# Attention and a softplus MLP in one kernel: eight heads of scores in one TensorE burst, the first loads over two DMA queues, and the order of work searched anew

## Chip, cores, metric

One Trainium2 chip, one core. The metric is the device time of one execution in microseconds (us), median over several. The span of a profile is some 2 us shorter than that time. The medians given beside them are of all runs; in numbers 1 to 4 below one run of the kernel before is a slow one, and in number 1 one of the edited kernel.

## The reference, cut

```python
# attention: batch 4, heads 8, sequence 768, head size 64; 8 global keys, window of 96
scores = scale * q @ k.T + bias(distance)          # keep: global or 0 <= rel < 96
a = softmax(where(keep, scores, -1e9));  x = a @ v
# the MLP on the 3072 x 512 result
h = x @ w_in                                       # 512 -> 2048
g = maximum(h, 0) + log1p(exp(-abs(h)))            # softplus
out = g @ w_out                                    # 2048 -> 512
```

## The kernel before: the parts that matter

The sequence is cut into 24 blocks of 128 queries (n = 0 to 23), two to a unit of loads and two to a group g of the MLP (12 groups). Every piece of work is an `op` with an engine, a planned duration, a rank, and what it reads and writes. A planner runs these through a small model, and its order is what each engine gets. So a changed number in the plan moves hundreds of instructions. The code is shortened.

```python
LEADS = {3: 2.25, 4: 2, 5: 3, ..., 9: 2, ...}       # how far ahead units are loaded
MARGIN = {-1: 15.0, 0: 13.5, 1: 25.5, 2: -36.5, 3: 1.5}
s_ps = [ps.tile([P, 2, 512], F32, name=f"s_ps{i}") for i in range(2)]   # 2 score tiles of 2 banks
# ...
def scores(n, part, rank):           # part: heads 0-3 or 4-7; 64 rows per matmul
    # ...
    for m in range(2):
        for u in range(u_all):       # own block, and the block before
            for y in range(2):
                # ... (rows: one half of the array; c: columns of the bank)
                nc.tensor.matmul(banks[:, y, c : c + P], kt[rows, 2 * part + m, :], qv(rows, 2 * part + m), ...)
# ...
def soften(n, part, rank):           # DVE adds the bias (z), ScalarE takes exp (pb)
# ...
def mm1(g, p, rank):                 # first product: 8 matmuls to h_ps; then e = exp(h), g = ln(1 + e) on ScalarE
def mm2(g, ns, rank):                # second product: g x w_out
# ...
for part in range(2):
    scores(n, part, rank + 0.1 * part)
    soften(n, part, rank + 0.1 * part)
```

Fillers are 90 matmuls on a blank tile, placed wherever the plan expects TensorE to be idle in the start. All loads are issued on SyncE.

The softmax here doesn't subtract the row's maximum and nothing guards it: scores larger than these inputs give would overflow.

Of the kernel before, what the change touches and what calls it, by code (L numbers as in the profile page):

```python
# [23 lines left out]
class Planner:  # L24
# [162 lines left out]

UNITS = [(0, 0), (1, 0), (0, 1), (0, 2), (1, 1), (1, 2), (2, 0), (2, 1), (2, 2), (3, 0), (3, 1), (3, 2)]
WIDE = (0, 1, 2)
FIRST_LOADS = "q1 k0 q0 i3 i6 i1 i0 k1 o0 i2 v0 v1 i7 i4 i5 o7 o2 q2 o1 o6 o3 o4 o5 k2 v2".split()  # L190
LOAD_LEAD = 2.5
LEADS = {3: 2.25, 4: 2, 5: 3, 6: 3, 7: 2.75, 8: 3, 9: 2, 10: 3.25, 11: 3.25}
FILLERS = 90
TABLE_RANK = -9000.0
BIAS0_ON = ["DVE"]
BIASA_ON = ["ACT"]
PE_BIAS = (0, 1, 3)
PE_KEYS = {
    0: (("o",), ("h0",), ("s", 1, 0), ("o",)),
    1: (("s", 1, 0), ("s", 1, 1), ("s", 1, 0), ("h0",)),  # L200
    2: (("s", 1, 0), ("s", 1, 1), ("x",), ("s", 1, 0)),
}
PE_X = {0: ("h1",), 1: ("o",), 2: ("o",), 3: ("o",), 4: ("x",), 5: ("x",)}
PV_KEYS = {
    (0, 0): ("h0",),
    (0, 1): ("o",),
    (1, 0): ("o",),
    (1, 1): ("h0",),
    (2, 0): ("o",),
    (2, 1): ("o",),  # L210
    (3, 0): ("o",),
    (3, 1): ("o",),
}
O_KEYS = {
    (0, 0): ("s", 1, 0),
    (0, 1): ("s", 0, 0),
    (1, 0): ("s", 1, 1),
    (1, 1): ("o",),
    (10, 1): ("x",),
    (11, 0): ("s", 1, 0),  # L220
}
FINE = 2
NARROW = ()
TAIL = 8.0
ENG = {
    0: {"k": ["POOL", "ACT"], "q": ["POOL", "POOL"], "tk": ["ACT", "ACT"], "tq": ["ACT", "DVE"], "v": ["POOL", "POOL", "DVE", "DVE"]},
    1: {"k": ["ACT", "POOL"], "q": ["DVE", "POOL"], "tk": ["DVE", "ACT"], "tq": ["ACT", "DVE"], "v": ["POOL", "ACT"]},
    2: {"k": ["POOL", "POOL"], "q": ["DVE", "POOL"], "tk": ["DVE", "DVE"], "tq": ["DVE", "ACT"], "v": ["ACT"]},
}
ENG_X = {0: "ACT"}  # L230
ENG_W = {"i3": "DVE"}
NUDGE = {
    "b0.0.10": -4,
    "b0.0.14": -0.5,
    "b0.0.2": -4,
    "b0.0.4": -8,
    "b0.0.6": -8,
    "b0.1.12": 2,
    "b0.1.2": 8,
    "b1.0.2": -4,  # L240
    "b1.1.12": -4,
    "biasTrue1": -8,
    "castk0.0": 4,
    "castk1.0": -4,
    "castk3.00": -8,
    "castk4.00": -2,
    "castq1.1": 4,
    "castq2.0": -2,
    "cin0": 8,
    "cin3": -8,  # L250
    "cpq0.0": 4,
    "cpq0.1": 1,
    "e0.0": 2,
    "e0.3": -8,
    "ex1.1": -4,
    "ldk3": -8,
    "ldk4": -2,
    "ldv4": 2,
    "nm2.0": 8,
    "nm2.1": 4,  # L260
    "nm3.0": -8,
    "nm3.1": -2,
    "pv3.0": 4,
    "sb0.1": -8,
    "sb1.1": -8,
    "sb3.1": -8,
    "sc3.0": -8,
    "sc3.1": 8,
    "trk1.0": -8,
    "wout4": 8,  # L270
    "xt2": -8,
    "xt3": -8,
}
DIST0_ON = "POOL"
S_ON = {
    (0, 0): 1,
    (0, 1): 1,
    (1, 0): 0,
    (1, 1): 0,
    (2, 0): 1,  # L280
    (2, 1): 0,
    (3, 0): 1,
    (3, 1): 0,
    (4, 0): 0,
    (4, 1): 1,
    (5, 0): 0,
    (5, 1): 0,
    (6, 0): 1,
    (6, 1): 1,
    (7, 0): 1,  # L290
    (7, 1): 0,
}
T0 = 47.5
LATER = 38.0
MARGIN = {-1: 15.0, 0: 13.5, 1: 25.5, 2: -36.5, 3: 1.5}
SOONER = {"cin": -36.0, "cout": 12.0}
LAST_KEYS = (("s", 0, 0), ("x",), ("o",))


@with_exitstack  # L300
def kernel(
# [129 lines left out]
    def load_unit(i, rank, only="qkv"):  # L431


        s, b0 = units[i][0]
        sl = slice(P * b0, P * b0 + W)
        for z, which in enumerate(only):
            src = {"q": q, "k": k, "v": v}[which][s]
            slot = raw_slot((which, i))
            raw = raw_t[slot]
            sync = gates.get((which, i), ())  # L440
            if i in WIDE and which != "v":
                for y in range(2):

                    def fn(src=src, raw=raw, y=y):
                        return nc.sync.dma_start(  # L445
                            raw[:, 512 * y : 512 * y + 512],
                            src[y::2, sl, :].rearrange("h (g r) d -> g h (r d)", r=8),
                        )

                    op(f"ld{which}{i}.{y}", "SP", 0.64, rank + 0.01 * z, fn, dma=(0.7, 86.0), sync=sync,  # L450
                       writes=[("raw", slot, y)])
                continue

            def fn(src=src, raw=raw):
                return nc.sync.dma_start(
                    raw[:].rearrange("p (h c) -> p h c", h=H),
                    src[:, sl, :].rearrange("h (p r) d -> p h (r d)", r=2),
                )

            op(f"ld{which}{i}", "SP", 0.45, rank + 0.01 * z, fn, dma=(1.78, 30.0), sync=sync,  # L460
               writes=raw_keys(slot))
# [111 lines left out]
    def transp_pe(i, which, banks, engs, rank):  # L573
# [4 lines left out]
        for rs in ((0, 1),) if len(held(banks)) == 1 else ((0,), (1,)):  # L578

            def mm(rs=rs):  # L580
# [4 lines left out]
                        nc.tensor.matmul(tr[:, a], src[:, c : c + P], ident[:])  # L585

            keys = held([banks[r] for r in rs])
            op(f"tr{which}{i}.{rs[0]}", "PE", 0.24 * len(rs), rank + 0.1 * rs[0], mm, count=4 * len(rs),
               reads=[(which + "b", i % NQB, x) for x in range(4)] + ["ident"], writes=keys)
            eng = engs[rs[0] % len(engs)]  # L590

# [44 lines left out]
               writes=[v_keys(prev)[r]], after=since)  # L636

    def s_of(n, part):
        return S_ON.get((n, part), part)

    def b_keys(n, part):
        return [("bias", blocks[n][1] > 0, h) for h in range(4 * part, 4 * part + 4)]

    def scores(n, part, rank):

        i = blocks[n][1]
        u_all = 2 if i > 0 else 1
        biased = n in PE_BIAS
        banks = s_ps[s_of(n, part)]
        key = ("s", s_of(n, part))  # L650
        qv = q_of(n)

        def seed():
            for y in range(2):
                src = (biasA if i else bias0)[:, part, 2 * u_all * y : 2 * u_all * y + 2 * u_all, :]
                nc.tensor.matmul(  # L656
                    banks[:, y, 0 : 256 * u_all], ident[:], src.rearrange("p a b -> p (a b)"),
                    start=True, stop=False, skip_group_check=True,
                )

        if biased:
            op(f"sb{n}.{part}", "PE", 0.22 * u_all, rank - 0.1, seed, reads=["ident"] + b_keys(n, part),
               writes=[key], count=2)

        def fn():
            for m in range(2):
                for u in range(u_all):
                    kt = kt_of(before(n) if u else n)
                    for y in range(2):
                        rows = slice(64 * y, 64 * y + 64)  # L670
                        c = P * (u_all * m + u)
                        reg = banks[:, y, c : c + P]
                        nc.tensor.matmul(  # L673
                            reg if unit_of(n) in WIDE else reg.rearrange("p (r t) -> p r t", r=2),
                            kt[rows, 2 * part + m, :], qv(rows, 2 * part + m),
                            start=not biased, stop=True, skip_group_check=biased,
                        )

        reads = kt_keys(n) + [("qT", unit_of(n) % NQT, r) for r in range(2)] + (kt_keys(before(n)) if i else [])
        op(f"sc{n}.{part}", "PE", 0.06 + 0.124 * u_all, rank, fn, reads=reads, writes=[key], count=4 * u_all)  # L680

    zi = {}

# [58 lines left out]
    def x_transp(n, key, eng, rank):  # L742
# [4 lines left out]
        if key is not None:  # L747
# [8 lines left out]
            def ev():  # L756
                copy_on[eng](dst, tr)

            op(f"xt{n}", "PE", 0.23, rank, mm, reads=in_keys + ["ident"], writes=held([key]), count=4)
            return op(f"xc{n}", eng, 0.36 if eng == "DVE" else 0.51, rank, ev, writes=[xkey] + held([key]))  # L760
        else:

# [112 lines left out]
                allow_small_or_imprecise_dtypes=True,  # L875
            )

    op("table", "ACT", 1.3, TABLE_RANK, table)
    op("blank", "DVE", 0.25, -9001.0, lambda: nc.vector.memset(blank[:], 0.0), writes=["blank"])  # L879
    op("iota", "POOL", 0.83, -9000.0, iotas, writes=["rel"], count=2)  # L880
    op("ident", "POOL", 0.6, -8999.0, lambda: make_identity(nc, ident), writes=["ident"], count=2)
# [27 lines left out]
    def biases(eng, late, h, rank):  # L909
        f = -slopes[h] * root_d  # L910
        part, at = h // 4, 2 * (h % 2) + h // 2 % 2
        dst, src = (biasA[:, part, 2 * at : 2 * at + 2, :], dist) if late else (bias0[:, part, at, :], dist0)

        def fn():
            if eng == "ACT":
                nc.scalar.mul(dst, src[:], f)
            else:
                (nc.vector if eng == "DVE" else nc.gpsimd).tensor_scalar_mul(dst, src[:], f)

        dur = {"DVE": (0.21, 0.30), "ACT": (0.20, 0.31), "POOL": (0.6, 0.9)}[eng][late]  # L920
        op(f"bias{late}{h}", eng, dur, rank, fn, reads=["dl0", "dl1"] if late else ["d0"],
           writes=[("bias", late, h)], port=eng == "DVE")

    distances(0, -9000.0)
    op("d0", DIST0_ON, 0.25, -8990.0, lambda: copy_on[DIST0_ON](dist0[:], dist[:, 0, :]), reads=["dl0"],
       writes=["d0"], port=DIST0_ON == "DVE")
    op("d0e", "DVE", 0.42, -8980.0, lambda: both(
        lambda sl: v_.tensor_scalar_min(dist0[sl, :], dist0[sl, :], float(NL))), writes=["d0"], count=2, port=True)
# [31 lines left out]
    def attend(n, rank):  # L960
        if blocks[n][1] >= 2:
            since = [placed[before(n)]] if before(n) in placed else []
            globals_k(n, rank, since)
            globals_v(n, rank + 0.3, since)
        for part in range(2):
            scores(n, part, rank + 0.1 * part)
            soften(n, part, rank + 0.1 * part)
        for part in range(2):
            pv(n, part, PV_KEYS.get((n, part), ("x",)), rank + 0.2)
        x_transp(n, PE_X.get(n), ENG_X.get(n, "DVE"), rank + 0.3)  # L970
# [134 lines left out]
```

## Time and profile before

225.42 us (three runs, 225.40 to 225.44).

| | before |
|---|---|
| span | 222.8 us |
| TensorE busy, fillers included | 216.6 us, 97% |
| ScalarE, DVE, POOL busy | 161.7, 107.2, 94.0 us |
| first transpose of q, first group of the first product | 7.55, 22.48 us |
| bursts of score matmuls | 35 |

The prediction below shows the lines and how they are read.

### The profile page before, as it was taken

What the parts mean: (1) busy time and instruction counts of PE and PEld (TensorE: products, weight loads), DVE (VectorE), ACT (ScalarE), POOL (GpSimd) and SP (SyncE); (2) the same over time, 40 slices, a digit from 0 to 9 for tenths busy, and PEclk for the clock granted to TensorE, in tenths of its full rate; (3) what the DMA queues carried; (4) which work ended last, traced back from release to release, by engine and by line L of the source; (5) the groups of instructions that cost most, each with busy time, mean ns of one, the idle gap of its engine ahead of it and who ended that gap; (6) DMA issues with size and microseconds to landing.
All of it is one profiled execution on the core that took longest, in us unless ns stands there. A gap on an engine that the chain in (4) does not pass through costs nothing.

```text
span 222.8 us, 5073 instructions
## 1 busy us (share of the span) xinstructions
PE 216.6 (97%) x2062; PEld 150.7 (68%) x2062; DVE 107.2 (48%) x205; ACT 161.7 (73%) x216; POOL 94.0 (42%) x157
## 2 busy tenths in 40 slices
PE   8899999999998999999999999999999999999994
PEld 5778897665574577767667676657667667767553
DVE  4246365560768767374266268118777621001121
ACT  5676889973399599897589587857987958877300
POOL 4457897593373836406445607748124100000000
PEclk9999999999999999999999999999999999999999
DMA  4999999975999487774999259996622131011112
GB/s 159 310 347 388 385 388 355 296 142 157 301 220 262 81 226 171 151 211 101 270 305 243 76 157 284 175 278 196 118 75 71 26 88 53 3 47 47 47 51 94
DMA packets 69847, 40.96 MB, mean 184 GB/s; under 512 B 30144, under 2 KB 61248, under 8 KB 69824
## 3 DMA queue, kind: packets, MB, share of 16 engines
q1 hardware_dynamic: 69680, 40.58, 69.5%
q8 instruction: 16, 0.26, 0.5%
q10 hardware_dynamic: 144, 0.07, 0.1%
q14 instruction: 7, 0.06, 0.1%
HBM read 27.26 MB, written 6.29 MB: 151 GB/s over the span
## 4 chain that ended last, share of the span: by engine, by line
PE 92%; ACT 2%; DMA 2%; POOL 1%; SPq 1%; DVE 0%; issue 0%
PE h_ps L779 38%; PE o_ps L828 27%; PE s_ps L828 7%; PE s_ps L673 6%; PE x_ps L722 4%; PE x_ps L940 3%; DMA raw<-in_q_dram 2%; PE x_ps L828 2%; PE s_ps L585 1%; ACT g L805 1%; ACT pb L705 1%; POOL vb L633 1%; PE s_ps L656 1%; SPq L445 1%; ACT e L794 1%; PE o_ps L722 1%
## 5 line engine op out<-in xcount | busy, mean ns | idle before, releaser
L779 PE MATMUL h_ps<-XT,w_in_bf 128*128 128x256 bf16 x768 | 96.7, 273 | 0.0
L779 PEld LDWEIGHTS <-w_in_bf 128*128 128x128 bf16 x768 | 72.5, 98 | 16.9
L794 ACT ACTIVATE e<-h_ps 128x512 f32<-128x512 f32 x96 | 59.7, 629 | 31.7 <-PE h_ps L779 31.2
L828 PE MATMUL o_ps<-w_out_bf,g 128*128 128x512 bf16 (+1 forms) x304 | 72.5, 371 | 1.0 <-ACT g L805 0.6
L828 PEld LDWEIGHTS <-g 128*128 128x128 bf16 x416 | 37.7, 98 | 32.5 <-ACT g L805 1.3
L698 DVE TENSOR_TENSOR z<-s_ps,biasA 128x1024 f32<-128x1024 f32 x36 | 43.2, 1220 | 21.5 <-PE s_ps L673 20.0
L805 ACT ACTIVATE g<-e 128x1024 bf16<-128x1024 f32 x48 | 50.7, 1057 | 1.3
L705 ACT ACTIVATE pb<-z 128x1024 bf16<-128x1024 f32 (+1 forms) x42 | 40.9, 987 | 9.0 <-DVE z L698 8.8
L857 DVE COPY osb<-o_ps 128x512 f32<-128x512 f32 (+1 forms) x19 | 12.7, 669 | 46.3 <-PE o_ps L828 46.2
L633 POOL COPY vb<-vb 4x512 bf16<-4x512 bf16 x32 | 20.1, 628 | 28.1 <-PE x_ps L722 27.1
L524 POOL CAST vb<-raw 64x512 bf16<-64x512 f32 x40 | 25.2, 631 | 14.9 <-DMA raw<-in_v_dram 13.3
L524 POOL CAST kb<-raw 64x512 bf16<-64x512 f32 x36 | 22.7, 631 | 20.0 <-DMA raw<-in_k_dram 18.5
L722 PEld LDWEIGHTS <-pb 128*128 128x128 bf16 x352 | 16.6, 98 | 5.3 <-issue 0.4
L733 DVE TENSOR_TENSOR xs<-x_ps,rcp 128x256 bf16<-128x256 f32 x40 | 17.0, 425 | 1.4
L828 PE MATMUL s_ps<-w_out_bf,g 128*128 128x512 bf16 (+1 forms) x80 | 17.0, 358 | 0.0
L722 PE MATMUL x_ps<-vb,pb 128*128 128x65 bf16 x304 | 16.0, 193 | 0.3 <-DVE xs L733 0.2
L940 PE MATMUL x_ps<-blank 128*128 128x256 bf16 x90 | 14.2, 307 | 1.1 <-DVE blank L879 1.1
L732 DVE RECIPROCAL rcp<-x_ps 128x4 f32<-128x4 f32 x40 | 7.1, 177 | 12.1 <-PE x_ps L722 12.1
L940 PEld LDWEIGHTS <-blank 128*128 128x128 bf16 x90 | 9.5, 113 | 3.1 <-DVE blank L879 1.1
L673 PE MATMUL s_ps<-qT,kT 64*128 64x128 bf16 x224 | 10.9, 218 | 0.0
L673 PEld LDWEIGHTS <-kT 64*128 64x128 bf16 x224 | 6.8, 94 | 5.7 <-issue 5.5
L482 POOL CAST w_out_bf<-raw 128x1024 bf16<-128x1024 f32 x8 | 8.3, 1040 | 3.3 <-DMA raw<-in_moe_w_out_dram 3.2
(72 smaller groups left out, 107.9 us busy)
## 6 DMA issues: line engine op xcount, KB each, us to landing
raw<-in_v_dram SPq DMA_DIRECT2D x12, 512.0 KB, 6.0
out_dram<-osb SPq DMA_DIRECT2D x23, 256.0 KB, 2.4
raw<-in_q_dram SPq DMA_DIRECT2D x9, 512.0 KB, 4.4
raw<-in_k_dram SPq DMA_DIRECT2D x9, 512.0 KB, 5.8
raw<-in_moe_w_in_dram SPq DMA_DIRECT2D x8, 512.0 KB, 10.3
raw<-in_moe_w_out_dram SPq DMA_DIRECT2D x8, 512.0 KB, 8.2
raw<-in_k_dram SPq DMA_DIRECT2D x6, 256.0 KB, 5.3
raw<-in_q_dram SPq DMA_DIRECT2D x6, 256.0 KB, 5.3
```

Source lines behind the costliest of these rows:

```text
L524: copy_on[eng](dst, src)
L633: nc.gpsimd.tensor_copy(vb_of(prev)[sl, :, 0:D], vb_of(first)[sl, :, 0:D])
L673: nc.tensor.matmul(reg if unit_of(n) in WIDE else reg.rearrange("p (r t) -> p r t", r=2), kt[rows, 2 * part + m, :], qv(rows, 2 * part + m ...
L698: nc.vector.tensor_tensor(z, src, bias, ALU.add)
L705: nc.scalar.activation(pb[:, 0:nr, :].rearrange("p (y a) b -> p y (a b)", y=2), src, AF.Exp, scale=1.0 / root_d)
L722: nc.tensor.matmul(xv[:, h, :], pb[:, u_all * (2 * (h % 2) + h // 2) + u, :], vb_of(prev if u else n)[:, 4 * part + h, :], start=u == 0, s ...
L733: nc.vector.tensor_tensor(xs[:, 4 * part : 4 * part + 4, :], xv[:, :, 0:D], rcp[:][:, :, None].to_broadcast([P, 4, D]), ALU.mult,)
L779: last = nc.tensor.matmul(hv[:, j, :], w_in_bf[:, m, fb * P : fb * P + P], XT[g % NXG][:, m, :], start=(m == 0), stop=(m == NM - 1),)
L794: nc.scalar.activation(e[:, p % 2, :, :].rearrange("p j (b t r) -> p (j b) r t", b=2, r=2), hb[:].rearrange("p (a r t) -> p a r t", a=4, r=2),
L805: nc.scalar.activation(gt[:, 2 * p - 2 : 2 * p + 2, :].rearrange("p a t -> p (a t)"), e[:].rearrange("p a j t -> p (a j t)"), AF.Ln, bias=1.0,
L828: nc.tensor.matmul(bank(key)[:, 0 : z - a], gt[:, fb, ns * P : ns * P + P], w_out_bf[:, fb, a:z], start=(fb == 0), stop=(fb == NFB - 1),)
L940: nc.tensor.matmul(x_ps[:, 0:256], blank[:, 0:P], blank[:, 0:256])
```

## The change

Intent: write the scores of 15 blocks for all eight heads at once, over both score tiles (four banks), so that TensorE changes its row tiling less often; and bring the first q in over ScalarE's queue while SyncE issues the first k and v. The plan's durations were refitted and its constants searched anew.

```diff
-    def scores(n, part, rank):
+    def scores(n, parts, rank):
...
+            for part in parts:
                 for m in range(2):
...
-        for part in range(2):
-            scores(n, part, rank + 0.1 * part)
-            soften(n, part, rank + 0.1 * part)
+        for parts in ((0, 1),) if n in WHOLE else ((0,), (1,)):
+            scores(n, parts, rank + 0.1 * parts[0])
+            for part in parts:
+                soften(n, part, rank + 0.1 * part)
...
+WHOLE = (0, 4, 6, 7, 8, 9, 10, 12, 13, 14, 15, 16, 17, 18, 23)
+LOAD_ON = {"q0": "ACT"}
...
-LEADS = {3: 2.25, 4: 2, 5: 3, 6: 3, 7: 2.75, 8: 3, 9: 2, 10: 3.25, 11: 3.25}
+LEADS = {3: 2.25, 4: 2.75, 5: 3, 6: 2.75, 7: 2.75, 8: 3.5, 9: 2.25, 10: 2.75, 11: 3.5}
-NARROW = ()
+NARROW = (0,)
-MARGIN = {-1: 15.0, 0: 13.5, 1: 25.5, 2: -36.5, 3: 1.5}
+MARGIN = {-1: 10.5, 0: -15.0, 1: 69.0, 2: 65.5, 3: 21.0}
... (engines of casts and copies, banks, some 200 small shifts of rank: cut)
```

## The prediction

> **What bounds the kernel now.** I read the page's busy table and its slices first, then the chain of waits, then timelines of TensorE, then the waits of the start.
>
> ```profile
> span 222.8 us, 5073 instructions
> PE 216.6 (97%) x2062; PEld 150.7 (68%) x2062; DVE 107.2 (48%) x205; ACT 161.7 (73%) x216; POOL 94.0 (42%) x157
> PEclk9999999999999999999999999999999999999999
> DMA  4999999975999487774999259996622131011112
> ...
> PE 92%; ACT 2%; DMA 2%; POOL 1%; SPq 1%; DVE 0%; issue 0%
> ...
> L940 PE MATMUL x_ps<-blank 128*128 128x256 bf16 x90 | 14.2, 307 | 1.1 <-DVE blank L879 1.1
> ```
>
> TensorE is busy 97% and carries 92% of the chain, at full clock throughout. The DMA engines are full for the first 8 slices of 5.57 us and rarely later. The last line is a warning: 90 of the matmuls multiply a blank tile. They are fillers that keep TensorE running while it has no work, so busy time hides idle time, and all of them lie in the start.
>
> I cut the span by stage. The chain of waits has its first useful matmul (a transpose of q) at 7.55 us and the first group of the first MoE product (8 matmuls to h_ps) at 22.55. A table by stage gives 14.9 of 14.9 us busy from 7.55 to 22.48, of which 62 fillers; back to back a filler takes 0.109 us in the chain ("0.87 ... x_ps L940 x8"), so 6.8 us of that stretch is idle time in disguise. From 22.48 to the last matmul at 219.7 TensorE counts 195.9 us busy of 197.2. The end, from 219.7 to 222.8, is one eviction and one store.
>
> So there are three places to gain: the start, whatever hides inside the busy 197 us, and a few true stalls. For the second, the timeline of TensorE in the middle (columns: start, duration, engine, what, count; a row's duration contains the modelled end of its last matmul, so I use differences of starts):
>
> ```profile
> 80.31 1.04 PE L779 MATMUL h_ps<-XT,w_in_bf 128*128 128x256 bf16 x8
> 81.28 0.40 PE L673 MATMUL s_ps<-qT,kT 64*128 64x128 bf16 x8
> 81.61 0.42 PE L722 MATMUL x_ps<-vb,pb 128*128 128x65 bf16 x8
> 81.87 1.04 PE L779 MATMUL h_ps<-XT,w_in_bf 128*128 128x256 bf16 x8
> 82.74 1.03 PE L828 MATMUL o_ps<-w_out_bf,g 128*128 128x512 bf16 x4
> 83.60 1.04 PE L779 MATMUL h_ps<-XT,w_in_bf 128*128 128x256 bf16 x8
> 84.57 0.62 PE L673 MATMUL s_ps<-qT,kT 64*128 64x128 bf16 x16
> 85.12 0.42 PE L722 MATMUL x_ps<-vb,pb 128*128 128x65 bf16 x8
> ```
>
> The reader is to see the price of entering and leaving the score matmuls. A group of 8 on L779 takes 0.87 us when another full-array group follows (81.87 to 82.74), but 0.97 when scores follow (80.31 to 81.28): 0.10 us to enter. Eight scores take 0.33 (81.28 to 81.61), sixteen take 0.55 (84.57 to 85.12): 0.22 for eight more, so 0.11 us to leave. Two bursts made one save 0.21 us.
>
> For the third, the only large true stall after the start is near 70 us:
>
> ```profile
> 66.67 1.98 ACT L705 ACTIVATE pb<-z 128x1024 bf16<-128x1024 f32 x2
> 68.55 1.04 ACT L805 ACTIVATE g<-e 128x1024 bf16<-128x1024 f32 x1
> 69.65 1.04 PE L828 MATMUL o_ps<-w_out_bf,g 128*128 128x512 bf16 x4
> 70.15 1.06 ACT L805 ACTIVATE g<-e 128x1024 bf16<-128x1024 f32 x1
> 71.26 1.04 PE L828 MATMUL o_ps<-w_out_bf,g 128*128 128x512 bf16 x4 [0.58 <-ACT g L805]
> ```
>
> ScalarE does the two exponentials of a block ahead of the logarithm that TensorE needs. TensorE's starts between 68.3 and 73.1 show about 1.8 us lost over what those matmuls take elsewhere.
>
> **What the Trainium skill says.** "TensorEngine Tiling (Array Packing)", section "Key Properties": changing the tiling mode drains TensorE. The scores use 64 rows and everything around them 128; the 0.10 + 0.11 us above agree. "TensorE: Matmul & The Clock Gate", Part 1, tells of a clock that needs work to stay up; the fillers are there for it, and the granted clock reads full in all slices. "DMA: Bandwidth & Descriptors", section "Issuing engines are not separate DMA queues": transfers from several engines share the same 16 DMA engines, so a second issuer saves only issue time. The trace of before has nearly all loads on one queue and cannot confirm it; it does show the issue time, 0.60 to 0.66 us per half tile.
>
> **The change part by part.**
>
> Scores in one burst. In 15 of 24 blocks the eight heads are written in one go, over both score tiles (four banks). That does not give 15 x 0.21 us: TensorE's timeline of before already has 10 bursts of sixteen where two halves happened to meet, beside 21 of eight, 3 of four and 1 of twelve, 35 bursts in all. After, 15 whole blocks plus 9 blocks in halves make at most 15 + 18 = 33; if a third of the nine pairs still meet, 30. 35 - 30 = 5 bursts x 0.21 = **1.0 us**, on the path, since TensorE has no other slack there (0.4 to 1.5 with 33 to 28 bursts). The matmuls themselves stay 352, and DVE's additions stay 36 of 1.22 us.
>
> The start. Loads in order of issue on SyncE:
>
> ```profile
> 0.73 0.66 SPq L445 DMA_DIRECT2D raw<-in_k_dram  x1
> 1.45 1.22 SPq L445 DMA_DIRECT2D raw<-in_q_dram  x2
> 2.71 1.25 SPq L445 DMA_DIRECT2D raw<-in_k_dram  x2
> 4.01 0.60 SPq L445 DMA_DIRECT2D raw<-in_q_dram  x1
> ...
> 5.95 0.60 SPq L455 DMA_DIRECT2D raw<-in_v_dram  x1
> 6.59 1.36 SPq L480 DMA_DIRECT2D raw<-in_moe_w_in_dram  x2
> ```
>
> q's second half is cast from 6.88, k's second used half from 7.60, v only at 12.46. With both halves of q on ScalarE, SyncE is spared two issues, 2 x 0.63 = 1.25 us, and q can start at 0.7 in place of 1.45. But q and k are 1 MB, and 310 to 390 GB/s (slices 1 to 5) carry 1 MB in about 3 us, so they cannot all be in before some 5.8: I take 1.0 us off the first transpose. ScalarE pays two issues of 0.6 us in a stretch where it waits for data anyway (1.9 us ahead of its first cast). The transposes of unit 0 also go to banks of their own (in before, o_ps serves q and then k, and the second k transposes start at 9.96 for that reason, 1.1 us after the first); some 0.7 us more. v earlier removes the wait of 2.7 us on DVE for it, which counts only as far as the exponentials (to 15.9) no longer cover it.
>
> The weights. In the first column chunk the loads become narrow: one 512 KB tile serves the first group instead of two, so TensorE can begin after 0.5 MB less, 0.5 / 0.385 = 1.3 us of a full DMA. In before the copy of XT ends at 19.95 while the casts of weights run until 21.7, so both the attention path and the weights must move, and I count the smaller: first h_ps group near 20, about 2.5 us earlier. Of that, scores and a bias seed that lay between 20.3 and 22.5 (1.5 us) must be done later, and half of those would fit a filler's place: **1.7 us** net. It is bounded by the 6.8 us of fillers.
>
> The new order of everything else (biases, casts, priorities) has no cost of its own. It can remove the 1.8 us near 70, or make such stalls elsewhere, since whole blocks bring the two exponentials (2.0 us) together more often. I put it at **0.5 us** gained. Sum: 1.0 + 1.7 + 0.5 = 3.2 us; 225.4 - 3.2 = 222.2 us.
>
> **The rivals.** (1) The start is bound by bytes. DMA is at 9 tenths from slice 1 and three units with both weights are 12.5 MB, 32 us at 385 GB/s; an earlier first group then waits for the following weights, and the gain is handed back as idle time between 25 and 40 us. For: the full DMA slices; against: TensorE had work throughout 22 to 44 us while the same bytes came in. It would leave 224. (2) Whole bursts need four free banks and hand ScalarE two exponentials in a row; logarithms come late and stalls like that at 70 us repeat. For: that stall; against: the eight other bursts of sixteen show no such gap. A few of 0.7 us would leave 224 to 226. (3) The reordering is better than I can see: start 3.5 us, bursts 1.5, stall all of 1.8 removed: 218.6.
>
> **Range and chances.** My terms run from 0.4 to 1.5, 0 to 3.5 and -1.5 to 1.8. Not all ends fall together, so 219.6 to 224.9 should hold eight times in ten, about 222.2. Two per cent lies at 220.9, 1.3 us beyond my figure, with a spread of some 2 us: 0.27 for faster. Slower by 2% would need 230, more than all rivals together: 0.04. The rest, 0.69, is within.
>
> **What would show it.** Right: about 30 score bursts, most of sixteen, still 0.10 and 0.11 us at the edges; first useful transpose near 6.5, first h_ps group near 20; fewer than 62 fillers' worth of time after the first transpose; no wait of TensorE for g near 70. Wrong: first group still near 22 (bytes or casts bind), filler time unchanged, or TensorE waiting for ScalarE's g or e several times. Busy time of DVE should stay near 107 us plus some casts, of ScalarE near 160; neither should become the bound.

## More of the kernel before

Later units load q and k, cast them to bf16 (mostly on POOL), and transpose them by DMA.

## The result, and the profile after

222.24 us (four runs, 221.98 to 222.85) against 225.43 us: ratio 0.9858, 95% interval 0.9835 to 0.9881. A ratio is the mean time of one kernel's fast runs over that of the other's of the same rounds, so not quite the ratio of the medians. Executions over 1.5% slower than the fastest of the same kernel are left out of the means. The change is 3.2 us faster, within 2%. On another chip the same kernel gave 0.9887 (0.9855 to 0.9918), number 5 below.

The page of the changed kernel, its busy times and its chain of waits:

```profile
span 219.9 us, 5042 instructions
PE 213.5 (97%) x2034; PEld 150.1 (68%) x2062; DVE 109.5 (50%) x204; ACT 160.1 (73%) x216; POOL 91.6 (42%) x156
...
PE 82%; DMA 10%; ACT 3%; SPq 3%; issue 1%; DVE 0%; ACTq 0%
```

TensorE is still the chain, with more of it in DMA and ScalarE. The matmul records lack 28 of 2062 here (the weight loads are complete), so busy times of TensorE can't be compared. I therefore compare **lost time**: at a moment t, t minus the standard times of all matmuls whose weight load has started. The standard times are the median spacings in the traces: 0.109 us for one of the first product or a transpose of q or k, 0.2157 for the second product, 0.029 for one with v, 0.028 for a score, 0.056 for a transpose of x, 0.2155 for a bias seed, 0 for a filler. Fillers, mode changes and stalls are all in it. The last column is the span minus the whole useful work (195.85 us).

| lost time, us, at | 22 | 34 | 65 | 80 | 140 | 160 | 200 | end | bursts |
|---|---|---|---|---|---|---|---|---|---|
| before | 14.3 | 14.7 | 16.3 | 18.6 | 21.8 | 22.7 | 23.3 | 27.0 | 35 |
| changed | 12.7 | 14.7 | 16.2 | 16.6 | 18.7 | 19.8 | 21.0 | 24.0 | 31 |
| changed, other chip | 13.0 | 14.9 | 16.4 | 17.6 | 19.3 | 20.5 | 21.7 | 24.9 | 31 |

Two traces of the changed kernel differ by up to 1.0 us, so single differences well under that are not secure. And the trace of before is of a run of 224.69 us, 0.7 below its median, so gains over it come out too small: 2.9 us of span here, 3.2 between the medians.

The first two rows say where the 3 us came from, and it isn't the start. At 22 us the change is 1.6 us ahead; at 34 us nothing is left of it. From 65 to 80 us it loses 0.4 us where before loses 2.3. From 80 to 140 it gains another 1.1, and there it starts 8 bursts where before starts 13: five at 0.21 us (the price found in the prediction) are 1.05.

**The start.** The timeline of the changed kernel (start, duration, engine, what):

```profile
0.73 0.64 ACTq L675 DMA_DIRECT2D raw<-in_q_dram  x1
0.73 1.55 SPq L675 DMA_DIRECT2D raw<-in_k_dram  x2
...
2.33 0.61 SPq L685 DMA_DIRECT2D raw<-in_v_dram  x1
...
6.53 0.61 PE L815 MATMUL h_ps<-ident,kb 128*128 128x128 bf16 x4
...
21.49 1.99 PE L1013 MATMUL h_ps<-XT,w_in_bf 128*128 128x256 bf16 x16
```

The first transpose comes 1.0 us earlier (7.55 to 6.53), the first group of the first product 1.0 us earlier (22.48 to 21.49). In the second trace they come at 7.17 and 21.77. There the 37 fillers that the order puts ahead of the first transpose end later: they start 0.213 us apart until 5.4 us and 0.109 after, in the first trace only until 4.0. So part of the 1.0 us is chance. Then it is given back, by waits that before hardly has there (same kernel, TensorE's timeline; the bracket is idle time and who ended it):

```profile
26.47 1.05 PE L1013 MATMUL h_ps<-XT,w_in_bf 128*128 128x256 bf16 x8 [0.33 <-POOL w_in_bf L712]
...
33.68 1.91 PE L1013 MATMUL h_ps<-XT,w_in_bf 128*128 128x256 bf16 x16 [0.25 <-ACT e L1028]
```

TensorE waits for the cast of a weight tile on POOL, and then for ScalarE, which puts two casts of v (31.72 to 32.97 us) ahead of an exponential that TensorE needs. In lost time the two are 0.52 and 0.21 us. From 22 to 34 us the changed kernel loses 2.0 us, before 0.4; most of the rest is five fillers, 0.8 us with the gaps around them, and a gap of 0.33 us before the transposes of q at 27.58.

**The bursts.** In the middle of the changed kernel:

```profile
76.57 1.91 PE L1013 MATMUL h_ps<-XT,w_in_bf 128*128 128x256 bf16 x16
78.41 0.62 PE L906 MATMUL s_ps<-qT,kT 64*128 64x128 bf16 x16
78.96 1.05 PE L1013 MATMUL h_ps<-XT,w_in_bf 128*128 128x256 bf16 x8
```

Sixteen full-array matmuls take 1.84 us up to the burst, where 16 x 0.109 = 1.74: 0.10 us to enter. The burst takes 0.55 us, 16 x 0.028 = 0.45 of it scores: 0.10 to leave. The price is as before; 31 bursts are left of 35.

**The stretch at 70 us.** A table by stage, one fence for each kernel: first before, then changed (PE is TensorE, PEld its weight loads, counts in brackets).

```profile
65.00:80.00 15.00, 13.87 (x154) 8.95 (x149) 11.61 (x19) 11.39 (x15) 8.05 (x15) 1.00 0.75 156
```

```profile
65.00:80.00 15.00, 14.90 (x168) 11.09 (x166) 8.97 (x16) 13.49 (x18) 7.73 (x14) 1.00 0.98 235
```

The same 15 us hold 149 weight loads before and 166 after. The idle time at 70 us is gone. TensorE's timeline of the changed kernel there:

```profile
67.30 1.67 PE L1062 MATMUL o_ps<-w_out_bf,g 128*128 128x512 bf16 x7
68.90 0.62 PE L906 MATMUL s_ps<-qT,kT 64*128 64x128 bf16 x16
...
71.44 1.04 PE L1013 MATMUL h_ps<-XT,w_in_bf 128*128 128x256 bf16 x8
```

After a group's last first product, ScalarE needs an exponential (0.6 us) and a logarithm (1.06 us) before the last second product can run. The changed kernel has two pieces of the second product still to do there and the next group's first product at 71.44. Before had done those pieces already, at 63.54 and 66.18, and its next first product came only at 77.0:

```profile
73.08 1.89 PE L828 MATMUL o_ps<-w_out_bf,g 128*128 128x512 bf16 x8 [0.23 <-DVE osb L857]
75.05 1.89 PE L828 MATMUL o_ps<-w_out_bf,g 128*128 128x512 bf16 x8
77.02 1.91 PE L779 MATMUL h_ps<-XT,w_in_bf 128*128 128x256 bf16 x16
```

These 16 second products, of the group's other block, were also still to do during the stall. They write the same o_ps bank as the half that waits for g, and come after it.

### The profile page after: what moved, and what is told of

The parts are those of the page before. It is cut to its first block, busy times and chain, and to the rows that moved or that the text cites. A ratio compares the mean times of both kernels' runs of the same rounds, so it can differ in the third digit from the quotient of the medians.

```text
span 219.9 us, 5042 instructions
## 1 busy us (share of the span) xinstructions
PE 213.5 (97%) x2034; PEld 150.1 (68%) x2062; DVE 109.5 (50%) x204; ACT 160.1 (73%) x216; POOL 91.6 (42%) x156
## 4 chain that ended last, share of the span: by engine, by line
PE 82%; DMA 10%; ACT 3%; SPq 3%; issue 1%; DVE 0%; ACTq 0%
PE h_ps L1013 35%; PE o_ps L1062 30%; PE s_ps L1062 5%; PE s_ps L906 5%; PE x_ps L956 5%; DMA raw<-in_moe_w_in_dram 4%; DMA raw<-in_k_dram 4%; DMA raw<-in_v_dram 2%; PE x_ps L1062 2%; SPq L710 2%; ACT e L1028 1%; ACT g L1039 1%; SPq L675 1%; ACT vb L754 1%; ACT kb L730 0%
## 5 line engine op out<-in xcount | busy, mean ns | idle before, releaser
L1062 PE MATMUL o_ps<-w_out_bf,g 128*128 128x512 bf16 (+1 forms) x296 | 74.1, 371 | 1.2
L754 POOL CAST vb<-raw 64x512 bf16<-64x512 f32 x44 | 27.5, 624 | 14.9 <-DMA raw<-in_v_dram 13.2
L1091 DVE COPY osb<-o_ps 128x512 f32<-128x512 f32 (+1 forms) x20 | 13.4, 670 | 38.2 <-PE o_ps L1062 38.0
L863 POOL COPY vb<-vb 4x512 bf16<-4x512 bf16 x32 | 19.9, 621 | 29.6 <-PE x_ps L956 26.3
L956 PEld LDWEIGHTS <-pb 128*128 128x128 bf16 x352 | 16.6, 98 | 5.8
L1174 PE MATMUL x_ps<-blank 128*128 128x256 bf16 x90 | 12.9, 295 | 1.1 <-DVE blank L1113 1.1
L1062 PE MATMUL s_ps<-w_out_bf,g 128*128 128x512 bf16 (+1 forms) x62 | 13.1, 352 | 0.1
L1174 PEld LDWEIGHTS <-blank 128*128 128x128 bf16 x90 | 9.0, 107 | 2.9 <-DVE blank L1113 1.0
L712 POOL CAST w_out_bf<-raw 128x1024 bf16<-128x1024 f32 x7 | 7.3, 1039 | 3.4 <-DMA raw<-in_moe_w_out_dram 3.4
```

Source lines behind the costliest of these rows:

```text
L754: copy_on[eng](dst, src)
L863: nc.gpsimd.tensor_copy(vb_of(prev)[sl, :, 0:D], vb_of(first)[sl, :, 0:D])
L956: nc.tensor.matmul(xv[:, h, :], pb[:, u_all * (2 * (h % 2) + h // 2) + u, :], vb_of(prev if u else n)[:, 4 * part + h, :], start=u == 0, s ...
L1062: nc.tensor.matmul(bank(key)[:, 0 : z - a], gt[:, fb, ns * P : ns * P + P], w_out_bf[:, fb, a:z], start=(fb == 0), stop=(fb == NFB - 1),)
L1174: nc.tensor.matmul(x_ps[:, 0:256], blank[:, 0:P], blank[:, 0:256])
```

## The experiments

Twelve kernels ran, numbers 1 to 4, 5 to 8 and 9 to 12 in one call and on one chip each (medians of before 225.10, 225.04 and 225.18 us); all gave the right result. In most of them the plan is left alone and only the order it put out is edited, by a helper that moves one operation ahead of another and then asserts that every operation still follows all that it depends on. So the other operations keep their order.

**1. Halves together in the kernel before.**

```diff
+    for n in range(NIT):       # 24 blocks
+        # move the second half of block n's scores (and its seeds) next to the first, if in_order()
+        joined(n)
```

> The kernel before, with only the second half of a block's scores moved next to the first on TensorE wherever its inputs and its bank allow it; all other engines keep their order. Bursts of scores go from 35 to 27. Theory (each burst costs 0.21 us to enter and leave, on the path): 8 x 0.21 = 1.7 us faster, 225.4 to about 223.7. Rival (the price is hidden by other waits, or moving the halves makes DVE and ScalarE late): within 0.5 us of before.

224.67 us against 225.10, ratio 0.9987 (0.9945 to 1.0030): nothing clear. But the lost time tells more: at 140 us it is 20.3 against 21.8 of before, 1.5 us ahead with 7 bursts fewer (21 against 28 by then), and 7 x 0.21 = 1.5. From 140 to 160 us it loses 2.5 us where before loses 0.9. Its timeline shows the place:

```profile
143.70 1.16 SPq L455 DMA_DIRECT2D raw<-in_v_dram  x2
...
144.95 3.15 SPq L611 DMA_TRANSPOSE kTa<-kb  x1
...
150.76 0.40 PE L673 MATMUL s_ps<-qT,kTa 64*128 64x128 bf16 x8 [1.62 <-DMA kTa<-kb]
```

The transpose of the last unit's k is issued behind two loads of v and needs 3.15 us to issue. In the kernel before the same transpose is issued at 144.43, takes 3.29 us, and TensorE comes to these scores at 150.44 without a wait. Both theories were half right: the price of a burst is real, and a later wait took it back. The total is also blurred by the clock. Two of its six runs show a granted clock of 0.991 and 0.992 and took 227.21 (the slow one) and 226.63 us; the other four took 223.64 to 224.78, on average 0.9 us less than before's fast runs.

**2. Whole bursts cut in two in the changed kernel, with a slip.** The next full-array operation was emitted between the halves, but the first half was emitted twice.

```diff
+    # for 14 blocks: emit half 0, the next TensorE operation x, half 1
+    o.fn = first;  x.fn = lambda: (first(), x(), second())    # the slip: first() again
```

> The changed kernel, with the burst of eight heads of 14 blocks cut in two by the TensorE operation that followed it; nothing else moves. Theory: 14 more bursts x 0.21 = 2.9 us slower, 222.2 to about 225.1. Rival (bursts are not what the time hangs on): within 0.7 us of the changed kernel.

228.62 us, ratio 1.0164 (1.0136 to 1.0192). That is too much for 14 bursts, and the trace shows 456 score matmuls in place of 352. It tests nothing cleanly and was repeated as number 6.

**3. The first q on SyncE again.**

```diff
-                        return dma_on[on].dma_start(
+                        return nc.sync.dma_start(
```

> The changed kernel, with the first q issued on SyncE again, all orders kept. Theory (what the start gains by 22 us is given back by 34 us, because weights, casts and ScalarE are the limit there): the first transposes come some 0.5 to 1 us later, the total stays within 0.4 us of 222.2. Rival (the start counts in full, as the prediction had it): 0.8 to 1.3 us slower.

227.26 us, ratio 1.0082 (1.0046 to 1.0117), some 5 us slower than the changed kernel. My theory missed by far, and so did its rival. The page has slices of 5.6 us:

```profile
PE   8399899999999999999999999999999999999995
...
PEclk9979999999999999999999999999999999999999
```

The order had left q's second half behind v and two halves of the next q. The transposes of q came at 10.62 us in place of 7.31, TensorE sat idle for 2.49 us because its order held no filler there, and in the third slice the granted clock fell: it was 0.50 from 10.7 to 14.1 us. Five of the six runs show a mean granted clock of 0.992 and took 226.68 to 227.42 us; the sixth shows 1.000 and took 225.12. So about 2 of the 5 us go with the clock.

**4. The first q on ScalarE's queue in the kernel before.**

```diff
+    for name in ("ldq0.0", "ldq0.1"):
+        put(name, "table")          # ahead of the table load, and issued on ScalarE
```

> The kernel before, with only the first q's two loads issued on ScalarE ahead of its table load; all else in the order of before. Theory: first transposes earlier, total within 0.4 us of 225.4. Rival: 0.8 to 1.3 us faster.

224.85 us against 225.10, ratio 0.9993 (0.9968 to 1.0019). The first transposes came at 6.85 in place of 7.55, the lost time is 0.7 us lower at 34 us and 0.9 at 140, and at 160 us 0.7 higher: a wait of 1.31 us for the same transpose of k at 151 us. The total is as the theory said, but for another reason: the start's gain lived to 140 us.

**5. The changed kernel again**, beside numbers 6 to 8.

> The changed kernel itself, unchanged, so that the runs beside it can be compared on the same chip. All theories: about 0.986 of the kernel before, 222 to 223 us.

222.51 us, ratio 0.9887.

**6. Whole bursts cut in two, cleanly.**

```diff
+    o.fn = first;  x.fn = lambda: (x(), second())
```

> The split of 14 whole bursts again, without the slip of the first try (there the first half of each was computed twice, so each cost eight more scores, some 0.22 us, as well). 31 bursts become 45, 352 score matmuls as in the changed kernel. Theory: 14 x 0.21 = 2.9 us slower than the changed kernel of the same call. Rival: the first try's 6 us came from disturbing the order, then this too is 5 us slower or more; or bursts are free, then under 0.7.

226.89 us, ratio 1.0071 (1.0037 to 1.0105), 4.4 us over the changed kernel. The trace has 352 scores in 45 bursts. The timeline shows one cut block:

```profile
59.28 0.40 PE L906 MATMUL s_ps<-qT,kT 64*128 64x128 bf16 x8
59.61 0.42 PE L958 MATMUL x_ps<-vb,pb 128*128 128x65 bf16 x8
59.96 0.40 PE L906 MATMUL s_ps<-qT,kT 64*128 64x128 bf16 x8
```

In the traces, lost time at 200 us is 25.0 against 21.7, 3.2 us for 14 bursts, 0.23 each (that profile is one of its faster runs); by the medians it is 0.31 each. So the mode change is paid on the path, at 0.21 us or somewhat more. What the rest is, perhaps the later softmax of the second half, I did not separate.

**7. The first q on SyncE, in good order.**

```diff
+    put("ldq0.1", "ldk0.0")     # q, k, q, k, v; all on SyncE
```

> The changed kernel with the first q on SyncE, but ahead of the first k's second half and of v, as the kernel before has it (the earlier try left q's second half behind v and two other loads). Everything later on SyncE comes two issues, some 1.25 us, later. Theory (the queue alone is worth little; what cost 5 us was q arriving 3 us late and the fillers running out): 0.3 to 1.2 us slower than the changed kernel. Rival (the ScalarE queue is what the gain rests on): 3 us or more slower.

223.45 us, ratio 0.9930 (0.9897 to 0.9964): 0.94 us slower than the changed kernel, as expected. The queue is worth about 0.9 us to this order; number 3's other 4 us were the order, the idle time it made and the clock that fell. Here the first transpose came only at 8.89 us, after an idle stretch of 2.03 us, but all six runs show a clock of 0.999 or 1.000.

**8 and 9. The remaining halves together in the changed kernel**, first all that can be (31 bursts to 25), then without block 3's (to 26).

```diff
+    for n in range(NIT):
+        if n not in WHOLE:                  # number 8;  number 9: and n >= 11
+            joined(n)
```

> The changed kernel, with the halves of the blocks that it still computes apart moved together where inputs and banks allow: 31 bursts become 25. Theory, if nothing downstream takes the gain: 6 x 0.21 = 1.3 us faster than the changed kernel. Rival (as in the kernel before with its halves moved together, a later wait for loads or transposes takes it back): within 0.4 us.

> The changed kernel with the halves of blocks 11 and 19 to 22 moved together (31 bursts to 26), but not block 3's, whose move delayed the start by some 1.4 us in the profiled run of the first try. Theory: 5 x 0.21 = 1.05 us faster than the changed kernel (222.5 on this kind of chip), 221.4, perhaps a little better than the first try's 221.6. Rival: equal to the first try or worse.

Number 8: 221.61 us, ratio 0.9839 (0.9804 to 0.9873), 0.9 us under the changed kernel. Its profiled run, at 223.06 its slowest, had lost 1.2 us more by 65 us than the changed kernel's trace: its first group comes at 22.11 in place of 21.77, and the next waits 0.83 us for the cast of a weight on DVE. Number 9, without the move of block 3, shows none of this. Number 9: 221.54 us, ratio 0.9851 (0.9821 to 0.9880). Its trace (span 219.0) follows the first trace of the changed kernel to within 0.1 us up to 140 us and is 1.0 us ahead at 200 us: 5 bursts, 0.20 us each. Here nothing takes the gain back. (Both traces are of the fastest runs of their kernels.) The medians of both are the lowest, but the intervals overlap those of the changed kernel, so "faster than it" rests on the trace and on number 8's neighbours.

**10. One margin of the plan changed in the kernel before.**

```diff
-MARGIN = {..., 3: 1.5}
+MARGIN = {..., 3: 15.0}
```

> The kernel before with one number of its plan changed (the margin by which the x of the fourth group is wanted ahead: 1.5 to 15; the change has 21), which puts first products of that group among the second products of the third. The plan shifts other work as well, so it is judged by the stretch from 65 to 80 us. Theory (TensorE stalls near 70 us because all that it has left there are second products that wait for ScalarE): time lost on TensorE between 65 and 80 us falls from 2.3 us to under 1. Rival (ScalarE's pairs of exponentials stall it whatever TensorE has to do): it stays near 2. The total may not follow, since a later wait can take it back.

226.02 us, ratio 1.0040 (1.0014 to 1.0066). From 65 to 80 us it loses 2.5 us, as much as before. The timeline there:

```profile
70.05 1.06 ACT L805 ACTIVATE g<-e 128x1024 bf16<-128x1024 f32 x1
71.16 1.04 PE L828 MATMUL o_ps<-w_out_bf,g 128*128 128x512 bf16 x4 [0.72 <-ACT g L805]
```

No exponential of scores stands between the logarithms any more, and still TensorE waits for g. The next group's first product came at 72.68, after the wait, not before it. So neither my theory nor its rival was put to a real test: the pairs of exponentials are not needed for the stall, but I did not manage to give TensorE other work at that moment.

**11 and 12. Halves together in the kernel before, with one transpose of k ahead of two loads of v; then the first q on ScalarE as well.**

```diff
+    put("trk9", "ldv9")
+    put("ldv10", "ldv9")        # SyncE: transpose of k (unit 9), then v 10, v 9
+    put("ldq0.0", "table"); put("ldq0.1", "table")      # number 12 only
```

> The kernel before with the halves of scores moved together (35 bursts to 27), as in the earlier run that gained only some 0.3 us, and with one transpose of k (unit 9) issued on SyncE ahead of two loads of v in place of behind them. Theory (that run had gained 1.5 us by 140 us and lost it to a wait of 1.6 us for this transpose at 150 us): the wait goes, total 1.5 to 1.8 us faster than before, 223.4. Rival (the gain is lost elsewhere, or the loads of v come late in turn): within 0.6 us of before.

> The same, and the first q's loads on ScalarE's queue as well. Theory: another 0.6 us (what q on ScalarE had gained by 140 us in the earlier run), so 2.2 us faster than before, 222.8. Rival: no more than the run without it.

224.37 us, ratio 0.9967 (0.9941 to 0.9992), and 223.92 us, ratio 0.9938 (0.9908 to 0.9968). Both theories (1.5 to 1.8 and 2.2 us faster) missed: the medians are 0.8 and 1.3 us under the 225.18 of before. At 140 us they have lost 19.9 and 19.7 us against 21.8 of before: the gains of bursts and start are there. At 160 us only 0.4 and 0.5 us are left in the traces. The transpose now issues in 1.26 us and the wait at 150 us is gone, but there is another (number 11):

```profile
144.43 1.20 SPq L455 DMA_DIRECT2D raw<-in_v_dram  x2
...
148.99 4.58 POOL L524 CAST vb<-raw 64x512 bf16<-64x512 f32 x7 [6.09 <-DMA raw<-in_v_dram]
...
157.68 0.23 PE L673 MATMUL s_ps<-qT,kTa 64*128 64x128 bf16 x2 [1.32 <-POOL kTa L624]
```

v came later, POOL's seven casts of it and five more casts ran until 157.3, and only then could POOL copy the global keys that the scores need. The rival (the loads of v come late in turn) is what happened. In the kernel before, the chain of the last two units, their loads, POOL's casts and the transposes, stands right behind TensorE between 145 and 160 us. In the traces of numbers 1, 4, 11 and 12 the stretch from 140 to 160 us takes back 1.5 to 1.7 us of what TensorE had gained earlier.

## Why the prediction was right, point by point

The total was right to 0.04 us, by sums that were partly right for the wrong reason.

- **The bursts** were predicted at 30 and 1.0 us. There are 31, so 4 x 0.21 = 0.84 us. The mechanism is shown from both sides: 14 bursts more cost 3.2 us in the trace and 4.4 in the median (number 6), 5 fewer save 1.0 us in the trace (number 9). What I did not see is that in the kernel before such a gain is lost at 150 us (numbers 1, 11), so the same step alone was worth a few tenths to 0.8 us.
- **The start** was the step that failed. The first transpose at 6.5 and 1.7 us less lost at 22 us came true in the first trace (6.53; 1.6 us), less so in the second (7.17; 1.3 us). What comes first is k, not q: q's transposes start at 7.31, 0.24 us earlier than in before. But unit 0's last ones start at 8.15 in place of 9.96, and 48 fillers in place of 62 lie between the first transpose and the first group, as foreseen. The first group of the first product was put near 20 and came at 21.49. And the 1.7 us were counted as net, as if no later stage could take them back, but at 34 us nothing is left. This is my first rival in part: it had the gain handed back between 25 and 40 us by weights that come late; the trace shows waits for a weight's cast on POOL and for ScalarE's e. Which of bytes, casts and order is the deeper cause I did not test. q's own queue is still worth 0.9 us to the new order (number 7); without it the new start would be slower than the old.
- **The reordering** was put at 0.5 us, with the stall near 70 us and new stalls netted. It was the largest term. From 65 to 80 us the changed kernel loses 1.9 us less in its first trace and 1.1 less in its second (0.2 of either is one burst fewer). My second rival, new stalls by pairs of exponentials, did not come. That the stall goes because TensorE has second products left over while ScalarE finishes the group is how the two timelines read; number 10 failed to show it by itself.
- **A reading that was off.** The page's row of the granted clock is full from the first slice, and I read it so. But before's fillers start 0.213 us apart until 5.29 us and 0.109 after. In number 3 fillers are 0.213 apart where the trace gives the clock as 0.50. The DMA engines, too, are at 4 tenths in the first slice. No term of my sum used either reading.
- **The end** has 0.4 us less between the last matmuls and the last store's landing, which no step had.

In the first trace: 0 for the start, 1.7 for the stretch at 70, 0.8 for bursts, 0.4 for the end, 2.9 us of span. (In the second, span and stretch give only 2.1 and 0.9.) The tenth of a microsecond in the forecast is luck; the start's 1.7 us too much and the reordering's 1.2 us too little cancelled.

One condition of the gain my prediction doesn't name: nothing waits at 150 us. From 140 to 160 us the changed kernel loses 1.0 us while it starts 5 bursts, which are all of it, and 2.9 of the 3.1 us gained by 140 us are still there at 160. That this is due to where its loads are placed is likely after numbers 1, 4, 11 and 12, but was not tested by itself.

## What to carry to other kernels

Count busy time on the bound engine as useful work at a standard time, and plot what is lost against the clock: it shows where a gain is made and where it is given back, when the total shows nothing. A saving on the bound engine can be lost again at the next place where a chain of loads, casts and transposes stands close behind it, so look for the waits that are just not there yet. Removing a change of TensorE's tiling mode gave 0.2 us each here, where nothing behind it took the gain back. What a late first load costs depends on the order around it: 5 us in number 3, with the clock's fall, and 0.9 us in number 7.

## What the Trainium skill lacked or had wrong

- "TensorEngine Tiling (Array Packing)", section "Key Properties", says that changing the mode drains TensorE, without a size. Here a burst of 64-row matmuls among 128-row ones costs 0.10 us to enter and 0.10 to 0.11 to leave; 14 more of them cost 3.2 us in the trace.
- "DMA: Bandwidth & Descriptors", section "Issuing engines are not separate DMA queues", calls the saved issue time usually small beside the DMA itself. Two issues of 0.6 us were worth 0.94 us of 222 in the changed kernel (number 7) and nothing in the kernel before (number 4), so what it is worth depends on what stands behind it.
- The same page's section on the DMA transpose does not tell how long its issue can take behind loads on the same queue. In number 1 the first transpose behind two loads of 512 KB took 3.15 us to issue; number 11 moved it ahead of them and it took 1.26 us, while the one now behind them took 3.13. Why was not tested.
- "TensorE: Matmul & The Clock Gate", Part 1, has the clock halved after at least one idle window of about 3.4 us. Number 3 shows the half clock (0.50 for 3.4 us), but no idle stretch of that length: 0.89 and 2.49 us, with four matmuls between them. One stretch of 2.03 us alone, in number 7, left the clock full.
